# Two weight loads of a spectral-mixing kernel, each split into half-row transfers of 64 rows and of 15 down to 1 rows

## The chip, the cores and the metric

The kernel runs on one core of a Trainium2 chip. The metric is the device time of one execution in microseconds (us). The kernel before has a median of 421.9 us over two runs (421.61 and 422.19).

## The reference

The first half is a linear attention: for each of 8 batches and 8 heads, `phi` is applied to q and k, `kv` is a 64x64 sum over 576 positions, and the rows are `phi(q) @ kv`, divided by `phi(q) @ z`. The second half takes these rows as x (8 batches, 576 positions, 512 channels):

```
X = np.fft.rfft(x, axis=1)
Xr, Xi = np.real(X[:, :64]), np.imag(X[:, :64])
Yr = np.einsum('bmd,mde->bme', Xr, w_r) - np.einsum('bmd,mde->bme', Xi, w_i)
Yi = np.einsum('bmd,mde->bme', Xr, w_i) + np.einsum('bmd,mde->bme', Xi, w_r)
Y[:, :64] = Yr + 1j * Yi
y = np.fft.irfft(Y, n=S, axis=1)
u = x + y
return u + np.maximum(u @ w_ch, 0.0)
```

So each of the 64 lowest frequencies ("modes") has two matrices of its own, `w_r[m]` and `w_i[m]`, each 512x512 in float32. Together they are 64 x 2 x 512 x 512 x 4 bytes = 134 MB, and each is used for 16 vectors only (8 batches, real and imaginary).

## The kernel before

**Weights.** Modes go in pairs: pair p holds modes 2p and 2p+1, and p runs from 0 to 31. A weight tile `w{p}` has 128 partitions and 16 x 512 elements in bfloat16, so 16 KB in each partition. Every even partition holds rows of `w_r`, every odd one rows of `w_i`: `w_load(p, half, ...)` (line 112) issues one transfer on the POOL queue for each of them, `half` 0 for `w_r` and 1 for `w_i`. Such a transfer has 64 rows of 8192 elements; it reads 2 MB of float32 and, converted on the way, writes 1 MB (16 KB into each of 64 partitions). Below, "8r" is the transfer of pair 8 with `half` 0 and "8i" the one with `half` 1.

**Buffers.** Pairs 0 and 1 go into two buffers that are kept (`wpool`, `W_KEEP = 2`), pairs 2 to 4 into three more (`W_PRE = 3`), which are given up after pair 4. From pair 5 on `w_get` (line 408) has `w_load` use the two kept buffers in turn, so the transfers of pair p are issued when the matmuls of pair p-2 have read their buffer. The last pair, 31, is loaded by `w_load_last` (line 122): three transfers of 512 KB and then five smaller ones (`PIECES`), so that its last matmuls can follow the data.

**Semaphores.** The transfers of the POOL queue tell of their landing on eight semaphores, in rotation. In the built program a transfer waits, before it is issued, until the one eight places before it on this queue has landed; where another wait already implies this, no separate one stands. POOL issues in program order (`pin`), so a transfer that waits holds up all that come after it.

**Mode pairs.** `mode_pair(p)` (line 462) runs 16 matmuls against the tile (`product`, line 432), copies the sum out of PSUM (`evacuate`: VectorE for even p, ScalarE for odd), transposes it with a selection matrix (`picks`, line 455), and does a share of other work from a list in between (`work_slot`): rows of the attention again, the inverse transform of the first 32 modes, and the products with `w_ch`. `keep_warm` (line 419) adds matmuls whose result isn't used.

**Around it.** Before the pairs, the attention and the forward transform run over the 8 batches, whose q, k and v come over the same POOL queue. After pair 31, the last mode's rows are added to all output tiles by `add_inverse` and `channels` (lines 760 and 800), and SP stores them.

Of the kernel before, what the change touches and what calls it, by code (L numbers as in the profile page):

```python
# [43 lines left out]
def kernel(  # L44
# [10 lines left out]
    nc = tc.nc  # L55
# [7 lines left out]
    NDW = 4 * NDC  # L63
    NDL = NDW // 2
# [41 lines left out]
    pin = tc.keep_in_program_order  # L106
    PIECES = (slice(0, 2), slice(2, 4), slice(4, 6), slice(6, 7), slice(7, 8))
    HALVES = [slice(0, 64), slice(64, 128)]

    LAST = NM // 2 - 1  # L110

    def w_load(p: int, half: int, pool, tag: str, bufs: int):
        if half == 0:
            w_in[p] = pool.tile([128, NDW, D], BF16, tag=tag, bufs=bufs, name=f"w{p}")
        two = (moe_w_r, moe_w_i)[half][2 * p : 2 * p + 2]
        pin(
            nc.gpsimd.dma_start(  # L117
                out=w_in[p][half::2], in_=two.rearrange("g (r dc) e -> (g r) dc e", dc=NDW)
            )
        )  # L120

    def w_load_last(pool, tag: str, bufs: int):
        w_in[LAST] = pool.tile([128, NDW, D], BF16, tag=tag, bufs=bufs, name=f"w{LAST}")
        for g in range(2):
            for half in range(2):
                rows_in = (moe_w_r, moe_w_i)[half][NM - 2 + g].rearrange("(p dc) e -> p dc e", dc=NDL)
                for dcs in PIECES if (g, half) == (1, 1) else (slice(0, NDL),):
                    dst = w_in[LAST][half::2, g * NDL + dcs.start : g * NDL + dcs.stop]
                    pin(nc.gpsimd.dma_start(out=dst, in_=rows_in[:, dcs, :]))
# [16 lines left out]
    def w_next():  # L146
        p, half = pending.pop(0)
        pool, tag, bufs = (wpool, "w", W_KEEP) if p < n_keep else (wpre, "wp", W_PRE)
        w_load(p, half, pool, tag, bufs)
# [258 lines left out]
    def w_get(p: int):  # L408
        if p not in w_in and p == LAST:
            w_load_last(wpool, "w", W_KEEP)  # L410
        elif p not in w_in:
            for half in range(2):
                w_load(p, half, wpool, "w", W_KEEP)
        return w_in[p]
# [14 lines left out]
    def product(P, x, n: int, w, dc: int, n_dc: int):  # L429
        c = dc % NDC * 32  # L430
        pin(
            nc.tensor.matmul(  # L432
                P[c : c + n, :], x, w[:, dc, :],
                start=(dc < NDC), stop=(dc >= n_dc - NDC), tile_position=(0, c),
                skip_group_check=True,
            )
        )

    def set_diagonal(p: int):
        for h in range(2):  # L440
            src = xt_v[HALVES[h], :, :, :, p].rearrange("p c t b -> p c (t b)")
            pin(nc.vector.tensor_copy(out=xz[p % 2][HALVES[h], :, h, :], in_=src))  # L442
# [19 lines left out]
    def mode_pair(p: int):  # L462
# [5 lines left out]
        for dc in range(NDW):  # L468
            product(P, xz[p % 2][:, dc].rearrange("p h n -> p (h n)"), 32, w, dc, NDW)
        if p + 1 < LAST:  # L470
            set_diagonal(p + 1)
# [15 lines left out]
    def last_pair():  # L487
        xl = ystage.tile([128, NDL, 2 * B], BF16, name="xl")
        for h in range(2):
            src = xt_v[:, (2 * h + 1) * NDC : (2 * h + 2) * NDC, :, :, LAST]  # L490
            pin(
# [3 lines left out]
            )  # L495
        w = w_get(LAST)
        kk = NM - 2
# [91 lines left out]
    def x_of(t: int):  # L589
        if t < B * NJJ:  # L590
            return x_main[t // NJJ][:, t % NJJ, :]
        i = t - B * NJJ
        return x_tail[i // 2][:, i % 2, :]
# [352 lines left out]
    for h, eng in enumerate((nc.sync, nc.gpsimd)):  # L946
        eng.dma_start(
            out=YZ_all[64 * h : 64 * h + 64 : NF // NL].rearrange("r b z d -> r b (z d)"),
            in_=last.rearrange("p z d -> p (z d)"),
# [15 lines left out]
    def sums_of(n: int, i: int):  # L965
# [8 lines left out]
            out=x_of(0), in0=accs[0][:, 0], scalar=0.0, in1=x_of(0), op0=ALU.max, op1=ALU.add  # L974
# [50 lines left out]
```

## Time and profile before

| what | value |
|---|---|
| median of the two runs | 421.9 us |
| span of the profiled execution | 419.4 us |
| TensorE (matmul) busy | 317.2 us, 76% |
| VectorE, ScalarE, POOL busy | 231.3, 154.2, 57.4 us |
| written by all transfers | 93.17 MB |
| read from HBM | 163.93 MB |
| first issue of 8r, 9r, 10r, 11r | 145.31, 155.90, 164.83, 174.47 us |
| matmuls of pair 31 end, stores begin | about 388, 391.6 us |

The span is the profiled execution from its first to its last instruction. What lies around it is the difference from a timed run, 421.61 - 419.4 = 2.2 us to 422.19 - 419.4 = 2.8 us; the median stands 2.5 us above the span. Times inside the execution are given from the start of the span. A DMA row names the queue that issued it and the time from issue to landing; a wait row names the engine and line that waited, what it waited for, the total, how often and the longest.

### The profile page before, as it was taken

The numbers are of one execution on the slowest core, as the hardware profiler recorded it, in microseconds if no ns is written. First come the engines' busy times: TensorE is split into PE (matmuls) and PEld (weight loads), VectorE is DVE, ScalarE is ACT, GpSimd is POOL, SyncE is SP. The second block draws the span as 40 slices with busy tenths as digits, with TensorE's granted clock in tenths as the row PEclk, the third lists the DMA queues.
The fourth block names the chain that finished last, engine by engine and source line by source line (L and its number), as shares of the span: only waits on it lengthen the run. The fifth ranks groups of instructions, "written<-read, shape, count | busy, mean of one in ns | idle before, by whom it ended". The sixth has DMA issues, their size and how long they took to land.

```text
span 419.4 us, 7466 instructions
## 1 busy us (share of the span) xinstructions
PE 317.2 (76%) x3143; PEld 164.4 (39%) x3143; DVE 231.3 (55%) x509; ACT 154.2 (37%) x253; POOL 57.4 (14%) x100
## 2 busy tenths in 40 slices
PE   0369998999617875676767686988798877998993
PEld 0257776877301332222222233433343332453421
DVE  4588899785314563463645353464456443522794
ACT  4677798854201011000000233334253432330783
POOL 4222224210011211111111111111111111130000
PEclk9999999579855658665655599899899997899998
DMA  8999999999999999999999999999999999998698
GB/s 217 211 212 216 210 222 203 228 206 223 217 223 208 218 220 209 220 217 212 220 214 213 223 213 214 223 210 216 220 209 219 217 214 219 216 209 166 235 391 328
DMA packets 17073, 93.17 MB, mean 222 GB/s; under 512 B 2112, under 2 KB 3024, under 8 KB 12880
## 3 DMA queue, kind: packets, MB, share of 16 engines
q0 software_dynamic: 12496, 81.48, 93.4%
q1 hardware_dynamic: 4544, 11.22, 7.2%
q8 instruction: 24, 0.39, 0.3%
q14 instruction: 9, 0.07, 0.0%
HBM read 163.93 MB, written 9.44 MB: 413 GB/s over the span
## 4 chain that ended last, share of the span: by engine, by line
DMA 64%; PE 23%; DVE 4%; POOL 3%; ACT 3%; issue 2%; DVEq 0%; ACTq 0%; POOLq 0%
DMA w<-in_moe_w_i_dram 53%; DMA pick_sb<-row_pick 8%; PE P L432 6%; DMA k<-in_k_dram 3%; PE acc L760 3%; PE kvp L257 3%; PE acc L800 2%; POOL w L117 2%; PE z L726 1%; DVE x L293 1%; ACT ke L208 1%; PE xf L355 1%; PE zl L419 1%; PE qTp L237 1%; PE num L163 1%
## 5 line engine op out<-in xcount | busy, mean ns | idle before, releaser
L432 PE MATMUL P<-w,xz 128*32 128x512 bf16 x496 | 42.6, 475 | 37.6 <-DMA w<-in_moe_w_i_dram 35.4
L419 PE MATMUL zl<-wch,id 128*128 128x512 f16 x185 | 58.2, 466 | 0.0
L449 ACT CAST ys<-P 128x512 f16<-128x512 f32 x15 | 8.8, 586 | 132.4 <-PE P L432 132.4
L117 POOL DMA_DIRECT2D w<-in_moe_w_r_dram x31 | 17.3, 559 | 246.4 <-PE P L432 211.8
L447 DVE CAST ys<-P 128x512 f16<-128x512 f32 x17 | 11.8, 692 | 51.0 <-PE P L432 51.0
L706 PE MATMUL eps<-wch,xTw 128*128 128x512 f16 x144 | 39.3, 399 | 0.0
L432 PEld LDWEIGHTS <-xz 128*32 128x32 bf16 x496 | 12.6, 108 | 63.3 <-DMA w<-in_moe_w_i_dram 40.3
L163 PEld LDWEIGHTS <-qT 64*128 64x128 f16 (+1 forms) x640 | 22.6, 122 | 29.6 <-issue 15.6
L689 ACT CAST x16w<-x_main 128x512 f16<-128x512 f32 x32 | 19.8, 618 | 37.8 <-DVE x_main L687 37.8
L687 DVE TENSOR_TENSOR x_main<-ya,x_main 128x512 f32<-128x512 f32 x32 | 22.0, 689 | 16.5 <-PE ya L683 16.3
L257 PE MATMUL kvp<-vpad,ke 32*128 32x130 f16 x576 | 24.3, 263 | 8.9 <-ACT qT L244 6.1
L442 DVE COPY xz<-xt_c 64x256 bf16<-64x256 bf16 x62 | 23.0, 371 | 10.9 <-PE P L432 10.0
L419 PEld LDWEIGHTS <-id 128*128 128x128 f16 x185 | 18.9, 112 | 25.6 <-issue 14.3
L714 ACT CAST E<-eps 128x512 f16<-128x512 f32 (+1 forms) x40 | 21.2, 540 | 17.7 <-PE eps L706 17.7
L257 PEld LDWEIGHTS <-ke 32*128 32x128 f16 x576 | 22.3, 116 | 10.6 <-issue 8.6
L163 PE MATMUL nw<-kv_sb,qT 64*128 64x65 f16 (+1 forms) x320 | 18.2, 231 | 9.8 <-DVE x_tail L650 4.7
L237 PE MATMUL qTp<-id,qe 128*128 128x128 f16 x144 | 15.1, 289 | 10.6 <-DVE qe L221 9.5
L293 DVE TENSOR_TENSOR x<-num,rd 128x512 f16<-128x512 f32 x32 | 22.1, 692 | 1.1
L650 DVE TENSOR_TENSOR x_main<-nw,rd 128x256 f32<-128x256 f32 x32 | 11.2, 416 | 18.8 <-PE nw L163 18.8
L455 PE MATMUL yt<-pick_sb,ys 128*128 128x32 f16 (+1 forms) x128 | 8.8, 185 | 16.7 <-DMA pick_sb<-row_pick 9.4
L698 DVE COPY xTw<-xTp 128x512 f16<-128x512 f16 x36 | 15.0, 416 | 10.3 <-PE xTp L696 10.3
L208 ACT ACTIVATE qe<-q 128x1152 f16<-128x1152 f16 (+1 forms) x16 | 17.9, 1157 | 7.2 <-DMA q<-in_q_dram 7.1
(118 smaller groups left out, 507.5 us busy)
## 6 DMA issues: line engine op xcount, KB each, us to landing
w<-in_moe_w_r_dram POOLq DMA_DIRECT2D x31, 1024.0 KB, 13.2
w<-in_moe_w_i_dram POOLq DMA_DIRECT2D x31, 1024.0 KB, 17.5
out_dram<-x_main SPq DMA_DIRECT2D x12, 512.0 KB, 3.6
k<-in_k_dram POOLq DMA_DIRECT2D x8, 576.0 KB, 12.9
v<-in_v_dram POOLq DMA_DIRECT2D x8, 576.0 KB, 14.3
q<-in_q_dram POOLq DMA_DIRECT2D x7, 576.0 KB, 12.6
out_dram<-x_main SPq DMA_DIRECT2D x8, 256.0 KB, 4.0
q<-in_q_dram SPq DMA_DIRECT2D x2, 576.0 KB, 4.5
```

Source lines behind the costliest of these rows:

```text
L117: nc.gpsimd.dma_start(out=w_in[p][half::2], in_=two.rearrange("g (r dc) e -> (g r) dc e", dc=NDW))
L163: mm = nc.tensor.matmul(num[hpo][orow, c0 : c0 + 65], qT[rows, hpp, h2, cols], kv_sb[rows, hpp, h2, :])
L208: pin(nc.scalar.activation(out=ev[:, c], in_=heads(nm, b, c), func=AF.Exp))
L257: nc.tensor.matmul(kv_ps[:, h2, 0:130], phi["k", b][r0 : r0 + 32, j // NJ, j % NJ].rearrange("p o d -> p (o d)"), vp[r0 : r0 + 32, :, j, 0 ...
L293: nc.vector.tensor_tensor(out=dst.rearrange("p (o c d) -> p o c d", o=2, c=4), in0=nv[:, :, :, 0:64], in1=rden.unsqueeze(3).broadcast_to([ ...
L419: pin(nc.tensor.matmul(last_ps[0], id16, wch16[:, 0, :]))
L432: nc.tensor.matmul(P[c : c + n, :], x, w[:, dc, :], start=(dc < NDC), stop=(dc >= n_dc - NDC), tile_position=(0, c), skip_group_check=True,)
L442: pin(nc.vector.tensor_copy(out=xz[p % 2][HALVES[h], :, h, :], in_=src))
L687: pin(nc.vector.tensor_tensor(out=x, in0=acc, in1=x, op=ALU.add))
L689: pin(nc.scalar.copy(out=x16w[t], in_=x))
L706: nc.tensor.matmul(e_ps, xT[:, c, :], wch16[:, c, :], start=(c == 0), stop=(c == NDC - 1))
L714: pin(nc.scalar.copy(out=dst, in_=e_ps[:, cols]))
```

## The change

A table `STAIRS` names two transfers, 8r and 10r. For these `w_load` no longer issues one transfer of 64 rows of 8192 elements. The rows are cut in two halves of 4096 elements (8 KB in each partition). The first halves of all 64 rows go as one transfer; the second halves go as a series of transfers of n rows each, with the n of the table, which add up to 64. All other transfers stay as they are, and so do the bytes, their places and the work of the other engines.

```
     LAST = NM // 2 - 1
+    STAIRS = {(8, 0): (15, 14, 13, 12, 10), (10, 0): (11, 9, 8, 7, 6, 5, 4, 3, 2, 1, 8)}
 
     def w_load(p: int, half: int, pool, tag: str, bufs: int):
         if half == 0:
             w_in[p] = pool.tile([128, NDW, D], BF16, tag=tag, bufs=bufs, name=f"w{p}")
         two = (moe_w_r, moe_w_i)[half][2 * p : 2 * p + 2]
-        pin(
-            nc.gpsimd.dma_start(
-                out=w_in[p][half::2], in_=two.rearrange("g (r dc) e -> (g r) dc e", dc=NDW)
-            )
-        )
+        rows_in = two.rearrange("g (r dc) e -> (g r) dc e", dc=NDW)
+        parts = [(0, 64, slice(0, NDW))]
+        if (p, half) in STAIRS:
+            parts, r0 = [(0, 64, slice(0, NDL))], 0
+            for n in STAIRS[p, half]:
+                parts.append((r0, r0 + n, slice(NDL, NDW)))
+                r0 += n
+        for r0, r1, dcs in parts:
+            dst = w_in[p][half + 2 * r0 : half + 2 * r1 - 1 : 2, dcs]
+            pin(nc.gpsimd.dma_start(out=dst, in_=rows_in[r0:r1, dcs]))
```

On POOL this makes 6 transfers of 8r and 12 of 10r, 16 more than before; the other engines have the same instructions in the same order. Below, 8a and 10a are the transfers of 64 half rows, and 8s1 to 8s5 and 10s1 to 10s11 the steps of the two stairs. The rotation of the semaphores now gives these waits on the queue, in its order, beside the wait of each pair's first transfer for its buffer:

| transfer | rows | waits for the landing of |
|---|---|---|
| 8a, 8s1 to 8s5 | 64, then 15, 14, 13, 12, 10 half rows | transfers from before 7r |
| 8i | 64 rows | 7r |
| 9r, 9i | 64 rows | 7i, 8a |
| 10a | 64 half rows | (its buffer's earlier contents: pair 8) |
| 10s1 to 10s5 | 11, 9, 8, 7, 6 half rows | transfers of pair 8 |
| 10s6 | 5 half rows | 9r |
| 10s7 | 4 half rows | 9i |
| 10s8 | 3 half rows | 10a |
| 10s9 | 2 half rows | 10s1 |
| 10s10 | 1 half row (as 16 pieces of 256 elements) | 10s2 |
| 10s11 | 8 half rows | 10s3 |
| 10i | 64 rows | 10s4 |
| 11r, 11i | 64 rows | 10s5 (and its buffer), 10s6 |

## Prediction

> **What bounds the kernel now.** First the page's slices, to see whether an engine or the transfers fill the span:
>
> ```profile
> PE   0369998999617875676767686988798877998993
> ...
> DMA  8999999999999999999999999999999999998698
> GB/s 217 211 212 216 210 222 203 228 206 223 217 223 208 218 220 209 220 217 212 220 214 213 223 213 214 223 210 216 220 209 219 217 214 219 216 209 166 235 391 328
> ```
>
> The 16 DMA engines are at 9 tenths or more from the second slice to the 36th and write some 216 GB/s throughout; TensorE is not. So the byte stream is the bound until pair 31 has landed, and the chain of waits says the same:
>
> ```profile
> DMA 64%; PE 23%; DVE 4%; POOL 3%; ACT 3%; issue 2%; DVEq 0%; ACTq 0%; POOLq 0%
> ```
>
> Then the chain in order of time around pairs 8 to 10, and POOL's issues there:
>
> ```profile
> 156.44 16.62 DMA w<-in_moe_w_i_dram
> 173.06 0.04 issue
> 173.11 1.05 PE P L432 x16
> ...
> 174.47 0.54 POOL w L117
> 175.01 17.46 DMA w<-in_moe_w_i_dram
> ```
>
> ```profile
> 145.31 0.54 POOL L117 DMA_DIRECT2D w<-in_moe_w_r_dram  x1 [5.54 <-PE nw L163]
> ...
> 155.90 0.54 POOL L117 DMA_DIRECT2D w<-in_moe_w_r_dram  x1 [9.51 <-PE P L432]
> ...
> 164.83 0.54 POOL L117 DMA_DIRECT2D w<-in_moe_w_r_dram  x1 [7.84 <-PE P L432]
> 165.37 0.54 POOL L117 DMA_DIRECT2D w<-in_moe_w_i_dram  x1
> ```
>
> The chain runs through one weight transfer after another, each with a short stretch of TensorE and POOL between. A transfer goes out ahead of need (10r at 164.83, while 9i lands only at 156.44 + 16.62 = 173.06), and that lead is all that keeps the engines fed: what costs time here is what lets their queues run dry.
>
> Two more facts decide. The first is that eight transfers may be out on this queue:
>
> ```profile
> 361.59 0.54 POOL L117 DMA_DIRECT2D w<-in_moe_w_r_dram  x1 [10.24 <-PE P L432]
> 362.13 0.55 POOL L117 DMA_DIRECT2D w<-in_moe_w_i_dram  x1
> 370.81 0.54 POOL L129 DMA_DIRECT2D w<-in_moe_w_r_dram  x1 [8.13 <-PE P L432]
> 371.35 0.54 POOL L129 DMA_DIRECT2D w<-in_moe_w_i_dram  x1
> 371.89 0.54 POOL L129 DMA_DIRECT2D w<-in_moe_w_r_dram  x1
> 372.44 2.17 POOL L129 DMA_DIRECT2D w<-in_moe_w_i_dram  x4
> 378.34 0.54 POOL L129 DMA_DIRECT2D w<-in_moe_w_i_dram  x1 [3.74 <-DMA w<-in_moe_w_i_dram]
> ```
>
> The last of these stood still for 3.74 us and went out 0.29 us after the landing at 378.05 of the transfer issued at 362.13, which is the eighth before it. The second is in the landing records, sixteen for each transfer, one from each DMA engine. They spread: the engines that are ahead land 9i at 170.81, the last one at 173.06 (2.25 apart); for the last piece of pair 31 it is 384.54 and 387.88 (3.34). The lag comes in steps of about 1 us and fits this row:
>
> ```profile
> q8 instruction: 24, 0.39, 0.3%
> ```
>
> Its 24 packets of 16 KB take 0.89 to 1.12 us each, and their durations repeat with period 8, so they fall on eight engines in turn. 23 come before the last weights land, 9 of these after 190 us. At the end eight engines are 2.2 to 3.3 us late and eight 0.0 to 0.5.
>
> **What one row costs.** Transfers of 1024 KB land 4.853 us apart and those of 512 KB in pair 31 2.445 us apart. With 4 rows on each engine, 8u + s = 4.853 and 4u + s = 2.445, so a half row takes an engine u = 0.602 us and each transfer s = 0.037 us more. (The pieces of 128 KB land 0.64 apart: u + s.)
>
> **The change, part by part.** Bytes are the same. Sixteen more transfers cost 16 x 0.037 = 0.6 us on each engine if none of it falls into a gap, and 16 x 0.54 = 8.6 us of POOL, which is idle for 8 to 10 us before every pair; this is at nothing as long as the queues hold, which is the point to test.
>
> *Stair of pair 8.* 8a goes out at 145.31, the steps from 145.85 to 148.0, and 8i waits for 7r (landed 148.82) and goes at 149.1, before 145.85. The engines that are ahead have 7i until 151.40 and the rows of 8r until 156.3. So 8i is there 7 us early: cost 5 x 0.037 = 0.19 us. 9i waits for 8a, which lands on the last engine 2.45 after 7i (153.65), at 156.1; 9i goes at 156.44 anyway.
>
> *Stair of pair 10.* 10a goes out at 164.83, 10s1 to 10s5 follow until 167.5, 10s6 after 9r (168.23) at 168.5. Then POOL stands still: 10s7 needs 9i, which lands on the last engine at 173.06 + 0.19 = 173.25, and goes at 173.25 + 0.29 = 173.54. 10s8 needs 10a: 173.25 + 2.45 = 175.70, issue 175.99. 10s9 needs 10s1: 175.70 + 0.64 = 176.34, issue 176.63. 10s10 follows 10s2, 0.64 later: 177.27; 10s11 0.54 after it at 177.81; 10i at 178.35. Before, 10i went out at 165.37, so the wait pushes it back 13 us, and behind it on POOL stand 11r and 11i (178.9 and 179.4, where they went at 174.47 and 175.01; early enough) and, on TensorE, the matmuls of pair 10.
>
> From issue to first packet: the POOL store of `last` is issued at 390.49 with empty queues and its first packet starts at 392.47, 1.98 us. The very first load (issued 1.25, packet at 5.48) took 4.2 us. I take 1.98, from the warm row, and keep 4.2 and, as the lower end, 0.5 (hardly more than the 0.54 of an issue). So 10i starts at 178.35 + 1.98 = 180.33. What can the engines do until then? If the stair's rows are spread evenly, 10a and 10s1 to 10s6 (46 of 64 rows, about 3 for each engine) keep the engines that are ahead until 173.26 + 0.3 + 3 x 0.64 = 175.5 and the last ones until 177.6; the remaining steps are 0.6 us of work. All sixteen are dry before 180.33. Before, 10i began on the engines ahead at 170.81 + 4.86 = 175.67: they lose 4.66 us. The last ones began at 177.89 and lose 2.4.
>
> *What comes back.* The gap lets the late engines catch up: all start 10i together, so the lag begins anew. After 190 us come 9 instruction packets on eight engines, so one engine gets two: 2 x 0.97 = 1.94 us at the end instead of 3.34. From the engines ahead: 4.66 + 1.94 - 3.34 = **+3.3 us** at the last weight. Behind it nothing changes (the tail from 388 to 419.4 is TensorE, VectorE and stores with their own chain). Span 419.4 + 3.3 = 422.7; the median stands 2.5 above the span, so **425.2 us**. With 0.5 us for the start it is +1.9, with 4.2 us +5.5.
>
> *Placement.* No transfer of fewer than 16 rows is in the trace, so where the rows go is bounded: evenly (above), always on the first n engines, or each transfer on one engine. On the first n: one engine gets 16 half rows of the two stairs instead of 8, 8 x 0.602 = 4.82 us; if it is one of the late ones, all of it comes on top of the old end (+4.8); if not, the gap decides, and since the stair of pair 8 gives the first ten engines one half row more, 9i and all that waits for it come 0.6 us later than above (some +4.0). I take even placement, since the rows of all other transfers land on sixteen engines within their lag.
>
> The Trainium skill, "DMA: Bandwidth & Descriptors", section "Why a DMA increments its semaphore by 16 and not by 1", says that a POOL transfer whose row count 16 doesn't divide runs on as many consecutive engines as the largest divisor up to 16, from a cursor that moves on, and also that some went to the first engines instead; the cursor gives the even case, +3.3, the exception the +4.0 to +4.8. Pair 31's pieces of 64 KB land 0.33 us apart, so a queued transfer of that size costs little beside its bytes. The same page, section "Rules for kernel authors", speaks against the change: merge small transfers, since under 64 KB one pays mostly overhead. By the fixed 2 us for each that the page's section "Anatomy of one DMA — SWDGE (gpsimd) path" gives, sixteen more in a row would be an estimated 32 us; that is no end of the range.
>
> **The rivals.** *Hidden:* the eight-deep wait has slack I don't see, and only s is left: 16 x 0.037 = +0.6 us, 422.5. The 3.74 us row speaks against it. *Faster, not slower:* the stair takes rows from the eight late engines and the queues don't run dry. If the shift met the lag exactly, all would end at the mean of the sixteen landings, 1.55 us after the first instead of 3.34: -1.8 us, 420.1. It decides if the late engines get at least 3 half rows fewer (3 x 0.602 = 1.8) and the wait of 10i costs under 1 us; the start of 180.33 speaks against that. *One engine at a time:* a step of 11 rows alone takes 11 x 0.60 = 6.6 us, and 10i waits for 10s4; 10s1 to 10s4 are 35 rows on up to four engines, 10s1 landing at 175.70 + 6.6 = 182.3. 10s9 goes at 182.6, and the three after it at 0.54: 10i at 184.2, first packet 186.2, 6 us after 180.33, so +9; with several steps on the same engine up to 6 more: +9 to +15, about 434. *Doesn't do what it says:* the engines run the stair as before, +0; the built program has the sixteen transfers and waits, so it has no chance of its own.
>
> **How the numbers follow.** Even placement 0.47 (+1.9 to +5.5); first n engines 0.25 (+4.0 to +6.4, the upper end with 4.2 us of start); hidden 0.10; one at a time 0.10; faster 0.08. The range leaves out the last two: from the hidden case to the first-n end, 422.4 to 428.4. A difference of 2%, 8.4 us, is taken as what a measurement can tell from no change: only one-at-a-time lies above (0.10), below there is at most an unseen gain (0.02), and 0.88 within.
>
> **What would show it.** Right: POOL's rows show 10s7 idle before a landing of `w`, 10i issued near 178; the slices show one dip of DMA at 176 to 180 us; pair 10 starts its matmuls near 185 (before 182.8); all later pairs are some 2 to 3.5 us late; landings of one transfer are within 0.5 us just after the gap and within 2 at the end. Wrong: no dip (hidden), landings that spread by 4 us or more after pair 10 (first n), or by over 6 (one engine), or an end before 387.9.

## The result and the profile after

The changed kernel has a median of 426.28 us over two runs (426.06 and 426.5) against 421.9: the ratio is 1.0107, with an interval of 1.0077 to 1.0136, so it is 4.4 us slower. The forecast was 425.2, in a range of 422.4 to 428.4. The profiled execution has a span of 424.7 us (before 419.4).

The slices of the page after, DMA share and GB/s:

```profile
DMA  8999999999999999799999999999999999998698
GB/s 218 211 212 215 211 218 207 226 210 221 222 212 222 217 211 216 131 205 215 215 218 216 216 215 218 218 214 215 219 218 211 216 219 219 210 213 164 228 388 326
```

One slice differs from before: the 17th (170 to 180 us), 131 GB/s where it was 220. All others until pair 31 stay between 205 and 226, where they lay between 203 and 228. The row of instruction packets, from the same page, is unchanged, and the share of DMA in the chain that ended last fell from 64% to 60%:

```profile
q8 instruction: 24, 0.39, 0.3%
```

```profile
DMA 60%; PE 24%; DVE 6%; ACT 3%; issue 3%; POOL 2%; DVEq 0%; ACTq 0%; POOLq 0%
```

POOL's rows of after show the wait that the prediction named (start, busy time, line, operation, count, and in brackets the idle time before and what ended it):

```profile
166.16 3.54 POOL L126 DMA_DIRECT2D w<-in_moe_w_r_dram  x7 [9.03 <-PE P L438]
173.89 0.50 POOL L126 DMA_DIRECT2D w<-in_moe_w_r_dram  x1 [4.19 <-DMA w<-in_moe_w_i_dram]
176.48 2.22 POOL L126 DMA_DIRECT2D w<-in_moe_w_r_dram  x4 [2.09 <-DMA w<-in_moe_w_r_dram]
178.85 0.55 POOL L126 DMA_DIRECT2D w<-in_moe_w_i_dram  x1 [0.15 <-issue]
179.73 0.55 POOL L126 DMA_DIRECT2D w<-in_moe_w_r_dram  x1 [0.32 <-PE nw L169]
```

The first row is 10a with 10s1 to 10s6. 10s7 waits 4.19 us for the landing of 9i (173.61), 10s8 another 2.09 us for that of 10a (176.20), and 10i goes out at 178.85, where it went at 165.37 before. TensorE's matmuls of pair 10 then start at 186.81 instead of 182.78:

```profile
186.81 1.90 PE L438 MATMUL P<-w,xz 128*32 128x512 bf16 x16 [4.24 <-DMA w<-in_moe_w_i_dram]
```

The chain in order of time must be read with care here (start, length, what):

```profile
156.59 17.02 DMA w<-in_moe_w_i_dram
173.61 0.04 issue
173.65 1.90 PE P L438 x15
175.55 0.39 PE nw L169 x8
...
179.73 0.54 POOL w L126
180.27 16.25 DMA w<-in_moe_w_i_dram
```

Between 173.61 and 179.73 it runs over TensorE and VectorE, because the last thing that 11r waited for was a matmul. But POOL's rows show that 11r waited only 0.32 us for it; the time before that was the wait of the stair. The chain names who came last for one instruction, not who let the DMA engines run dry.

How much was lost can be read from windows of 5 us. Of before, and then of after (window; busy time of the engines, TensorE's granted clock, DMA share, GB/s):

```profile
core 0: us, PE busy (x) PEld busy (x) DVE busy (x) ACT busy (x) POOL busy (x), PEclk, DMA share, GB/s
...
170.00:175.00 5.00, 2.19 (x34) 0.82 (x33) 0.56 (x2) 0.59 (x1) 0.53 (x1) 0.84 1.00 213
175.00:180.00 5.00, 3.82 (x33) 1.88 (x33) 4.30 (x16) 0.00 (x0) 0.56 (x2) 0.50 1.06 226
180.00:185.00 5.00, 2.82 (x39) 1.02 (x37) 1.58 (x5) 0.00 (x0) 0.85 (x2) 0.84 1.02 216
```

```profile
170.00:175.00 5.00, 3.22 (x21) 0.87 (x19) 0.33 (x1) 0.00 (x0) 0.50 (x1) 0.50 0.83 172
175.00:180.00 5.00, 3.58 (x54) 1.97 (x47) 3.44 (x12) 0.59 (x1) 2.83 (x6) 0.50 0.46 77
180.00:185.00 5.00, 2.57 (x7) 0.61 (x4) 1.90 (x7) 0.00 (x0) 0.81 (x2) 0.70 1.04 197
```

The last column is short by 41, 149 and 19 GB/s, together 209. Times 5 us, over a stream of 216 GB/s, that is 4.8 us of bytes not moved. The last weight landed at 392.78 instead of 387.88, 4.90 later. So nearly all of the loss arose between 170 and 185 us, and nothing later gave it back.

### The profile page after: what moved, and what is told of

It is laid out like the page before. It is cut to its first block, busy times and chain, and to the rows that moved or that the text cites. A ratio compares the mean times of both kernels' runs of the same rounds, so it can differ in the third digit from the quotient of the medians.

```text
span 424.7 us, 7491 instructions
## 1 busy us (share of the span) xinstructions
PE 317.2 (75%) x3143; PEld 161.9 (38%) x3143; DVE 230.9 (54%) x509; ACT 154.0 (36%) x253; POOL 65.6 (15%) x116
## 4 chain that ended last, share of the span: by engine, by line
DMA 60%; PE 24%; DVE 6%; ACT 3%; issue 3%; POOL 2%; DVEq 0%; ACTq 0%; POOLq 0%
DMA w<-in_moe_w_i_dram 49%; DMA pick_sb<-row_pick 8%; PE P L438 7%; DMA k<-in_k_dram 3%; PE acc L766 3%; PE zl L425 2%; PE kvp L263 2%; PE acc L806 2%; POOL w L126 1%; DVE x L299 1%; PE eps L712 1%; ACT qT L250 1%; PE qTp L243 1%; PE yt L461 1%; ACT ys L455 1%
## 5 line engine op out<-in xcount | busy, mean ns | idle before, releaser
L438 PE MATMUL P<-w,xz 128*32 128x512 bf16 x496 | 47.5, 522 | 38.0 <-DMA w<-in_moe_w_i_dram 35.8
L126 POOL DMA_DIRECT2D w<-in_moe_w_r_dram x47 | 25.1, 537 | 240.0 <-PE P L438 223.4
L425 PE MATMUL zl<-wch,id 128*128 128x512 f16 x185 | 59.8, 476 | 0.0
L712 PE MATMUL eps<-wch,xTw 128*128 128x512 f16 x144 | 40.8, 411 | 0.0
L263 PE MATMUL kvp<-vpad,ke 32*128 32x130 f16 x576 | 23.3, 254 | 7.8 <-ACT qT L250 4.9
L263 PEld LDWEIGHTS <-ke 32*128 32x128 f16 x576 | 21.4, 112 | 9.3 <-issue 6.8
L243 PE MATMUL qTp<-id,qe 128*128 128x128 f16 x144 | 13.2, 266 | 13.2 <-DVE qe L227 9.7
L169 PE MATMUL num<-kv_sb,qT 64*128 64x65 f16 (+1 forms) x320 | 16.0, 212 | 6.6 <-DVE x L299 3.9
```

Of the source, the lines that this page charges most:

```text
L126: pin(nc.gpsimd.dma_start(out=dst, in_=rows_in[r0:r1, dcs]))
L169: mm = nc.tensor.matmul(num[hpo][orow, c0 : c0 + 65], qT[rows, hpp, h2, cols], kv_sb[rows, hpp, h2, :])
L263: nc.tensor.matmul(kv_ps[:, h2, 0:130], phi["k", b][r0 : r0 + 32, j // NJ, j % NJ].rearrange("p o d -> p (o d)"), vp[r0 : r0 + 32, :, j, 0 ...
L425: pin(nc.tensor.matmul(last_ps[0], id16, wch16[:, 0, :]))
L438: nc.tensor.matmul(P[c : c + n, :], x, w[:, dc, :], start=(dc < NDC), stop=(dc >= n_dc - NDC), tile_position=(0, c), skip_group_check=True,)
L712: nc.tensor.matmul(e_ps, xT[:, c, :], wch16[:, c, :], start=(c == 0), stop=(c == NDC - 1))
```

## The experiments

Each kernel below was timed beside the kernel before on the same chip, whose median was 421.50 us for e1 to e4, 421.20 for e5 to e8 and 421.56 for e9 and e10; each difference below is from that one. Three theories were set against each other. *Dry queue*: the eight-deep wait holds 10i back and the engines run dry. *Uneven rows*: a transfer of n rows goes to the first n engines, so that some of them get more than their share and end later. *Fixed price*: each extra transfer costs the same, 4.38 / 16 = 0.27 us.

### One stair alone (e1, e2)

```diff
-    STAIRS = {(8, 0): (15, 14, 13, 12, 10), (10, 0): (11, 9, 8, 7, 6, 5, 4, 3, 2, 1, 8)}
+    STAIRS = {(8, 0): (15, 14, 13, 12, 10)}                        # e1
+    STAIRS = {(10, 0): (11, 9, 8, 7, 6, 5, 4, 3, 2, 1, 8)}         # e2
```

> Only the stair of pair 8 (5 of the 16 added transfers, none of which waits for anything late). Against the kernel before, 421.9 us. Dry queue (the loss is the gap that the eight-deep wait leaves before 10i): +0.2 to +0.3 us. Uneven rows (transfers of fewer than 16 rows go to the first engines, so that some engines have more to carry): +0.6 to +0.8, one half row for the first ten engines. Fixed price (4.4 us / 16 = 0.27 us for each transfer): +1.4. Landings: even placement keeps the spread of a transfer at 2.5 us after the stair; uneven rows put one engine about 2.4 us ahead.

> Only the stair of pair 10 (11 of the 16 transfers, with all of the late waits). Dry queue: +3 to +4 us, nearly all of the loss. Uneven rows: +3.5 to +4.2 (7 half rows more on the first engine, 4.2 us). Fixed price: 11 x 0.27 = +3.0.

e1: 422.33, +0.83 us, ratio 1.0020 (1.0012 to 1.0029). e2: 425.42, +3.92, 1.0100 (1.0085 to 1.0115). The stair of pair 10 brings nearly all of the loss, which dry queue and uneven rows had both expected. In e1 nothing runs dry:

```profile
175.00:180.00 5.00, 3.59 (x54) 1.98 (x47) 3.55 (x12) 0.58 (x1) 1.08 (x2) 0.50 1.01 213
```

Its +0.83 fits uneven rows. The landing records show it: the sixteen landings of 8a are 2.34 us apart, those of 8i after the five steps 4.88, and for 8s1 to 8s5 one engine reports at 154.23, 154.40, 154.58, 154.74, 154.91. Any engine with a row would be 0.6 us later, so it is the same one five times, and it has nothing to move. (The records don't name the engines. Shown is that this one is left out each time; that n rows always go to the same first n is the simplest reading of it.) The five steps have 64 rows in all, so if each step had gone on where the one before ended, every engine would have got four.

### Whole-height pieces with the same waits (e3)

The second halves are cut along the columns, each piece with all 64 rows. Numbers of transfers, their order and their waits are those of the change (units of 256 elements).

```diff
-    STAIRS = {(8, 0): (15, 14, 13, 12, 10), (10, 0): (11, 9, 8, 7, 6, 5, 4, 3, 2, 1, 8)}
+    PARTS_OF = {(8, 0): (4, 4, 4, 2, 2), (10, 0): (2, 2, 2, 2, 2, 1, 1, 1, 1, 1, 1)}
...
+                dcs = slice(c0 // 2, max(c0 // 2 + 1, (c0 + n) // 2))
+                cols = slice(0, D) if n > 1 else slice(c0 % 2 * 256, c0 % 2 * 256 + 256)
+                parts.append((rows[:, dcs, cols], rows_in[:, dcs, cols]))
```

> The same count of transfers at the same places with the same waits, but each of 64 rows and a part of the columns (5 parts of 8r's second half, 11 of 10r's), so that every engine has four pieces of each and no engine has more than another. Dry queue: the gap before 10i stays, +3.4 to +4.4 us. Uneven rows: nothing is uneven, 16 x 0.04 = +0.6. Fixed price: +4.4.

425.60, +4.10, ratio 1.0106 (1.0089 to 1.0124). Its POOL rows have the same two waits:

```profile
173.62 0.54 POOL L128 DMA_DIRECT2D w<-in_moe_w_r_dram  x1 [3.75 <-DMA w<-in_moe_w_i_dram]
176.06 2.18 POOL L128 DMA_DIRECT2D w<-in_moe_w_r_dram  x4 [1.89 <-DMA w<-in_moe_w_r_dram]
178.21 0.58 POOL L128 DMA_DIRECT2D w<-in_moe_w_i_dram  x1
```

The landings of 8a to 10s6 stay 2.5 to 2.6 apart (2.2 to 2.3 in the kernel before), and the loss is there all the same. Uneven rows aren't needed for it; the wait is enough. The profile is of the slowest run of e3 (427.86 us; the other four took 425.1 to 426.0). Its last weight landed at 392.74, 4.86 us later than before. The rest lies behind that: at a granted clock of 0.50 from 388 to 390 us, where after has 1.00, TensorE ended the last matmuls on the weights 2.0 us after the landing instead of 0.3.

### 10i ahead of the wait (e4, e5)

e4 is the changed kernel with 10i issued after 10s5 and the last six steps behind it; e5 does the same with the pieces of e3. Rows, bytes and numbers of transfers stay as they are.

```diff
+        if len(parts) > 6:
+            parts, held[p] = parts[:6], parts[6:]
...
-            for half in range(2):
-                w_load(p, half, wpool, "w", W_KEEP)
+            w_load(p, 0, wpool, "w", W_KEEP)
+            late = held.pop(p, [])
+            w_load(p, 1, wpool, "w", W_KEEP)
+            for dst, rows_of_part in late:
+                pin(nc.gpsimd.dma_start(out=dst, in_=rows_of_part))
```

> Both stairs as in the changed kernel, but 10i is issued after the fifth step of its stair; the last six steps follow it. 10i then waits for 9r alone and goes out near 169, before the queues are dry; all rows, sizes and counts are the same. Dry queue: the gap is gone, +0.6 to +1.6 us. Uneven rows: +4.8 if the engine with 8 half rows more is one of the late ones, +1.9 if it is one of the early ones. Fixed price: +4.4.

> Neither the gap nor the unevenness: the pieces of e3 (64 rows each, 16 transfers more than before) in the order of e4 (10i after the fifth piece). Dry queue: +0.6 us, 16 x 0.04. Uneven rows: also +0.6, so that e4 minus e5 (2.45 measured for e4) is the price of the uneven rows, +1.9 us. Fixed price for each transfer: +4.4.

e4: 423.95, +2.45, ratio 1.0057 (1.0045 to 1.0069). e5: 421.87, +0.67, 1.0015 (1.0006 to 1.0024). POOL's rows of e4:

```profile
166.31 3.02 POOL L132 DMA_DIRECT2D w<-in_moe_w_r_dram  x6 [9.11 <-PE P L447]
169.32 0.57 POOL L132 DMA_DIRECT2D w<-in_moe_w_i_dram  x1
174.01 0.51 POOL L428 DMA_DIRECT2D w<-in_moe_w_r_dram  x1 [4.12 <-DMA w<-in_moe_w_i_dram]
176.50 2.60 POOL L428 DMA_DIRECT2D w<-in_moe_w_r_dram  x5 [1.98 <-DMA w<-in_moe_w_r_dram]
...
183.41 0.54 POOL L132 DMA_DIRECT2D w<-in_moe_w_i_dram  x1 [3.76 <-DMA w<-in_moe_w_i_dram]
```

The waits of 4.12 and 1.98 us are still there, but 10i is out at 169.32, before them, and its 1 MB keeps the engines busy meanwhile. What counts is how many bytes are queued ahead of a wait, not its length. e5 has all sixteen extra transfers, no dry engines and no uneven rows: +0.67 is at most what their number costs, 0.04 us each, and the fixed price (+4.4) is dead. Two differences follow: e3 - e5 = 3.4 us for the dry queue, and e4 - e5 = 1.8 us for the stairs in place of even pieces. The second isn't the price of uneven rows alone, and e4's +2.45 is more than dry queue had expected of it (0.6 to 1.6). In both kernels the six late pieces only move the wait on: now 11i stands still for the landing of 10i, for 3.76 us in e4 (the last row above) and 3.87 in e5, and goes out at 183.41 and 182.97 instead of 175.01. From 185 to 190 us e4 then moves 184 GB/s, where e5 moves 210 and the kernel before 223. Against the kernel before that is another 0.9 us of bytes in e4 and 0.3 in e5.

### Rows taken off the last eight engines (e6, e7)

If the late engines lay together, steps of 8 or 7 rows, which go to the first engines, could level the lag and gain time.

```diff
+    ROWS_OF = {(p, 0): (48, 8, 8) for p in (8, 12, 16)}             # e6, full rows
+    ROWS_OF = {(12, 0): (48, 7, 7, 1, 1)}                           # e7, full rows
```

> Placement by itself, without a late wait: the transfers 8r, 12r and 16r (whole rows) are each divided into 48, 8 and 8 rows, 6 transfers more than before. If a transfer of 8 rows goes to the first eight engines, these carry 5 rows instead of 4 each time and the others 3, 3 x 1.2 = 3.6 us apart from the mean by the end: +3.8 us if one of the first eight is a late one (three instruction packets), +0.9 if all late ones are among the last eight. If the 8 rows go to eight engines in turn, both halves get the same: +0.3. Fixed price: 6 x 0.27 = +1.6.

> One transfer, 12r, divided into 48, 7, 7, 1 and 1 rows: by the rule of the first n engines the first seven carry one row (1.2 us) more and the other nine 0.9 to 1.0 less; a single row is split over all sixteen. If the late engines are all behind the first seven, as the landings of e1 suggest, the last landing comes earlier: -0.6 us. If a late one is among the first seven: +1.5. Rows in turn: +0.2. Fixed price: +1.1.

e6: 425.77, +4.57, ratio 1.0112 (1.0098 to 1.0126). e7: 422.87, +1.67, 1.0039 (1.0026 to 1.0052). Both are slower, by about what was expected if a late engine is among the first eight (3.8), and among the first seven too (1.5). In e6 the sixteen landings of 12i spread over 6.8 us. The records don't name the engines, so which ones are late stays open; no stair that would pay was found.

### How many pieces the lead allows (e8, e9)

e3 with the second half of 10r in seven pieces, and in six. One piece more moves 10i from the eighth place behind 9i to the eighth behind 10a.

```diff
-    PARTS_OF = {(8, 0): (4, 4, 4, 2, 2), (10, 0): (2, 2, 2, 2, 2, 1, 1, 1, 1, 1, 1)}
+    PARTS_OF = {(8, 0): (4, 4, 4, 2, 2), (10, 0): (4, 2, 2, 2, 2, 2, 2)}        # e8
+    PARTS_OF = {(8, 0): (4, 4, 4, 2, 2), (10, 0): (4, 4, 2, 2, 2, 2)}           # e9
```

> As e3, but the second half of 10r in 7 pieces of 64 rows instead of 11 (12 transfers more than before instead of 16). 10i then waits for 10a alone, near 176.1, first packet near 177.5, where the late engines are dry only at 177.9. Dry queue: only the engines ahead lose time, which they have, +0.3 to +0.8 us, though e3 with four transfers more lost 4.1. Uneven rows: +0.5. Fixed price: 12 x 0.27 = +3.2.

> The even pieces of e3, with the second half of 10r in six pieces (4, 4, 2, 2, 2, 2 units) instead of seven or eleven: the transfer that stands eight places before 10i is now 9i, not 10a. Dry queue: 10i goes out about 0.3 us after the landing of 9i, near 173.7, its first packets come near 175.4, before the engines ahead are done with 10r at 175.8; no dip, and only the pieces' own cost is left: +0.5 us (0.2 to 0.9). A fixed price of 0.27 us for each of the 11 extra transfers: +3.0. If the +1.8 with seven pieces was not the wait but something that grows with pieces: about +1.6.

e8: 423.01, +1.81, ratio 1.0044 (1.0032 to 1.0057), of which dry queue had expected only 0.3 to 0.8. e9: 421.87, +0.31, 1.0009 (1.0000 to 1.0018), as it said. POOL's rows of e8, then of e9:

```profile
173.56 0.54 POOL L128 DMA_DIRECT2D w<-in_moe_w_r_dram  x1 [3.75 <-DMA w<-in_moe_w_i_dram]
176.01 0.54 POOL L128 DMA_DIRECT2D w<-in_moe_w_i_dram  x1 [1.90 <-DMA w<-in_moe_w_r_dram]
```

```profile
165.97 3.89 POOL L128 DMA_DIRECT2D w<-in_moe_w_r_dram  x7 [9.09 <-PE nw L171]
173.61 0.54 POOL L128 DMA_DIRECT2D w<-in_moe_w_i_dram  x1 [3.75 <-DMA w<-in_moe_w_i_dram]
```

In e9 10i goes out at 173.61, 2.3 us before the engines that are ahead are done with 10r (175.90). In e8 it goes at 176.01, when they have just run dry (175.78), and its first packet comes at 177.26. So the edge lies between six and seven pieces: one piece more costs 1.5 us. What e8's expectation left out is that the first packets then take longer, told below.

### Two stairs without a late wait (e10)

```diff
+    STAIRS = {(8, 0): (15, 14, 13, 12, 10), (10, 0): (15, 14, 13, 12, 10)}
```

> Both pairs with the five-step stair 15, 14, 13, 12, 10, so that 10i waits for a transfer of pair 8 or 9r only and no queue runs dry. Uneven rows on the first n engines: the first ten engines carry one half row more for each of the two stairs, 2 x 0.60 us on a late engine, and 10 transfers more: twice the +0.83 of one such stair, +1.4 to +1.8 us. Even placement: 10 x 0.037 to 10 x 0.05, +0.4 to +0.5. A fixed price of 0.27 us each: +2.7.

422.95, +1.39, ratio 1.0035 (1.0021 to 1.0048). 10i waits only for 9r and is out at 168.85. The first such stair cost 0.83 (e1), so the second costs 0.56 more, and the landings of 10i are 6.9 us apart. Uneven rows add up as long as nothing runs dry.

### The bytes missing from 170 to 185 us

The reading from the windows of after, made for each run but e6 and e7, which change later pairs: GB/s in the three windows, what they lack against 213, 226 and 216, times 5 / 216.

| kernel | GB/s in the three windows | bytes missing, as us | measured, us |
|---|---|---|---|
| after | 172, 77, 197 | 4.8 | +4.4 |
| e2, stair of pair 10 | 189, 107, 174 | 4.3 | +3.9 |
| e3, whole-height pieces | 191, 111, 167 | 4.3 | +4.1 |
| e8, seven pieces | 194, 163, 213 | 2.0 | +1.8 |
| e5, 10i ahead, whole height | 212, 204, 213 | 0.6 | +0.7 |
| e9, six pieces | 194, 226, 213 | 0.5 | +0.3 |
| e4, 10i ahead, stairs | 205, 194, 211 | 1.0 | +2.5 |
| e10, two stairs of five | 195, 213, 213 | 0.8 | +1.4 |
| e1, stair of pair 8 | 220, 213, 213 | 0.2 | +0.8 |

Where rows are even or a gap opens, the missing bytes are the loss within 0.4 us. In e4, e10 and e1 they aren't: there most engines stay busy, but some have more to do than others, which shows in the spread of the landings, and e4 loses another 0.9 us after 185 us. The DMA share misleads in such a comparison, since small packets keep an engine busy with few bytes: e3 has a share of 0.87 from 175 to 180 us at 111 GB/s.

## Why the prediction was right, and where it wasn't

**The sign, the mechanism and its place were right.** The stream bounds the kernel; 10s7 waits for 9i, 10s8 for 10a, 10i stands behind them, and the engines run dry. e2 puts the loss at the stair of pair 10, and two pairs of runs take it away by what 10i waits for: e5 is e3 with 10i ahead of the wait and loses 3.4 us less, e9 is e8 with one piece less and loses 1.5 less. POOL grew by 65.6 - 57.4 = 8.2 us (forecast 8.6). It grew by 66.2 - 57.4 = 8.8 in e5 too, where the sixteen transfers cost 0.67 us in all (forecast 0.6).

**The start of 10i was right by two errors.** The issue was expected at 178.35 and came at 178.85: the stair of pair 8 spread the engines, so that the last one landed 9i at 173.61 instead of 173.25. The first packet came 1.38 us after the issue, not 1.98. The sum is 180.23 against 180.33, so the hit was luck.

**Two terms were too small.** First, the engine that is ahead landed 10i 5.39 us later than before (185.91 against 180.52), where the sum has 4.66. The packets of the two traces show where the 0.73 comes from. The sum set the first packet of 10i (180.33) against a landing, that of 10r at 175.67; but a landing stands some 0.3 us behind the end of its last packet, and in the kernel before this engine had begun 10i at 175.39, 0.28 us earlier. In after the engine that landed 10i first began it at 180.50, 0.17 later than the forecast. And its first packet took 1.44 us, where the same packets take 1.23 later on: 0.21. The last 0.07 is a landing 0.35 us behind its packet instead of 0.28. On the other engines the first packets took up to 2.40 us; in e8 it was 1.37 to 2.42 and in e3 1.57 to 2.39 on all engines but one, and in e9 10i began with 1.23 to 1.51.

Second, "the lag begins anew, 1.94 at the end" left out the spread that the gap leaves: 10i landed over 0.86 us, and the end shows 2.84 = 0.86 + 1.98. The last weight by the measured terms: engines ahead 389.94 - 384.54 = +5.40, spread 2.84 - 3.34 = -0.50, together +4.90 against +3.3. The signs named for it were too small as well: pair 10 started its matmuls at 186.81, not near 185, 4.0 us late instead of 2 to 3.5, and the landings were 0.86 us apart after the gap (0.5) and 2.84 at the end (2).

**Two more terms, and luck.** Behind the last weight 0.4 us more came (31.92 us to the end instead of 31.52), which was taken as nothing. Most of it is TensorE's: in the kernel before it waited for the last pieces and ended its matmuls on them 0.32 us after the last landing; in after it worked without a pause from 389 us on and ended them 0.60 after it (393.38). The other way, what lies around the span was taken as 2.5 us. It is 1.7 to 1.8 in both runs of after (426.5 - 424.7 and 426.06 - 424.3), and in every other run for which time and span of the same execution are on record, 47 of the kernel before among them. The 2.5 set the span of one execution, 419.4, against the times of two others, whose own spans were then some 419.8 and 420.4. By luck this error took 0.7 us off the miss of the sum. That the two timed runs of before lay high may also be why bytes and last weight say 4.8 to 4.9 us and the times 4.4: against the medians of the kernel before that stand beside the experiments (421.20 to 421.56), 426.28 is 4.7 to 5.1 more.

**Readings of the prediction that don't hold.** At the end nine engines are 2.2 to 3.3 us late and seven 0.0 to 0.5, not eight and eight; the instruction packets, on eight engines, leave the ninth open. The mean of the sixteen landings lies 1.76 us after the first, not 1.55, so the best that *faster* could have gained was 1.6 us, not 1.8. With 0.5 us for the start the sum gives +1.8, not +1.9.

**The step that failed is "I take even placement".** Steps of fewer than 16 rows go to the first n engines: e1's idle engine and the spread from 2.34 to 4.88 show it, e6 and e10 confirm it. The first-n case, +4.0 to +4.8, holds the measured +4.4. Yet in after uneven rows are not what costs: e3 without them loses 4.1. So the even case had the right mechanism with the wrong placement, and the first-n case the right number without the right reason. When 10i comes, the engines have run dry and start it within 1.3 us of each other, from 180.23 to 181.46 (landings 6.5 us apart at 10s6, 0.86 at 10i), so the gap swallows what the rows made uneven. The mark "spread of 4 us or more after pair 10" for the first-n case was therefore badly chosen: it has to be read before the gap.

The Trainium skill, "DMA: Bandwidth & Descriptors", section "Why a DMA increments its semaphore by 16 and not by 1", gives both cases, the moving cursor and, as an exception for some copies, rows handed out from engine 0 on. The transfers here behave as in the exception: e1 shows an idle engine through five steps, where a cursor that goes on from step to step would have given each engine four rows.

**The rivals.** *Hidden* (+0.6) is what e5 shows when the wait is out of the way, so the wait is the price. *Faster* needed steps that spare the late engines; e6 and e7 show late ones among the first engines. *One engine at a time* is out: steps of 15 to 10 rows in e1 cost 0.83 us in all.

The rule of the same page, section "Rules for kernel authors", to merge small transfers holds here for another reason than their overhead. e5 issues sixteen more, six of them of only 32 KB, for 0.67 us; what costs is that each of them takes one of eight places on the queue.

**What stays open.** Why first packets take longer isn't settled. Each run that let the engines run dry shows it, but a dry spell isn't needed: in e4 and e5, where 11i goes out late, packets from 185.3 us on took up to 2.76 and 2.65 us on engines that had work until then.

## What to carry to other kernels

Before a transfer is split on a queue that allows a fixed number in flight, count which landing the transfer behind the pieces will wait for, and whether the bytes queued before it last until then; six pieces cost 0.3 us here, seven 1.8 and eleven 4.1. Where more pieces are wanted, issue the next large transfer ahead of those that must wait. Cut along the columns, with all rows in each piece.

## What the runs showed that was not expected

- An engine without rows in a transfer still takes 0.17 us for it (the five landings of e1), more than four times the 0.037 us that a transfer costs an engine which has rows.
- A gap realigns the engines. The landings of the transfer behind it are 0.9 us apart in after, e2 and e3, and 2.2 apart in the kernel before at the same place.
- Pair 9's matmuls took 1.90 us in after and 1.05 in the kernel before, at a granted clock of 0.50 instead of 0.84 (windows of 170 to 175 us). They took 1.90 in e9 as well, which loses 0.3 us in all: there, beside the stream of weights, the slower TensorE cost at most that.
